# Attention into a squared-ReLU MLP on one core: contiguous scores in the first softmax, a single expansion of p for the late batches, and a new order of the work

## The chip, the cores and the metric

The kernel runs on one core of a Trainium2 chip. The metric is the device time of one execution in microseconds. Before the change, three runs took 312.1, 312.61 and 314.21 us; the median is 312.61 us. A profile of one further execution gives the durations used below.

## The reference

All inputs and the output are float32. There are 8 batches of 8 heads, 576 tokens, head dimension 64, and 32 packed queries `p` per head.

```python
def sm_attn(qq, kk, vv):
    s = scale * qq @ kk.T          # scale = 1/8
    a = exp(s - max(s)); a = a / (sum(a) + 1e-9)
    return a @ vv
p_packed = sm_attn(p, k, v)              # 32 packed queries over 576 keys
out = sm_attn(q, p_packed, p_packed)     # 576 queries over 32 packed keys
x = out.transpose(0, 2, 1, 3).reshape(4608, 512)
h = maximum(x @ w_in, 0)                 # 512 -> 2048
return (h * h) @ w_out                   # 2048 -> 512
```

## The kernel before, in words

**Steps of a batch.** GpSimd (POOL) issues all loads; they convert float32 to bfloat16 on the way. VectorE (DVE) transposes k and q in 32x32 blocks (`tr_k`, `tr_q`: Tk, Tq) and regroups v (`group`: G). Four heads are stacked on the 128 partitions; a `qd` is such a group of four heads, so a batch has two. `expand_p` (X) spreads the transposed p over a block-diagonal tile `pT_bd`, so that one matmul serves four heads.

S1 (`s1`, L467) multiplies p and k into PSUM, 128 rows by 576 scores. `s1_max` (L473, L474) takes the maximum and scales it, `s1_exp` (L481) does the exponential in two instructions (five and four groups of 32 keys a side) and spreads the result into the order in which v lies, with zeros behind it up to 640 columns. `s1_norm` (L489 to L491) adds the two sums, inverts them and normalises. E (`s1_tr`, `s1_out`: L496) transposes the result on PE and copies it out; PV (L509) multiplies it with v. XT copies the packed result out of PSUM twice: block-diagonally into `pq_bd` (`pq_block`) as the keys of the second attention, and into `ppT` (`extract`).

M (L532) multiplies the packed result with w_in, before the second attention's weights are applied; so the MLP's first product becomes a product of M and the attention weights. S2 (L553, and L560 for the last 64 tokens, `s2_rest`) computes the second attention's scores; L572 to L595 are its softmax; N (L602, L605) transposes it. F1 (L618) multiplies M and the weights in 16 blocks of 128 hidden units; each is rectified (L630 on ScalarE, or ACT; L632 on DVE) and squared (L640, or L638) into `gT`. F2 (L648) multiplies gT and w_out in 36 tiles of 128 tokens with 16 matmuls each; a tile is copied to `o_sb` and stored through the SyncE queue. L387 and L389 are the lines of the helper `cast`, which copies on ACT and on DVE.

**PSUM.** There are four tiles `ps0` to `ps3` of two banks each. S1, F1 and the large S2 take a whole tile (`HB`: ps0 or ps1). E, PV, the small S2 and N take one half of ps2 (`AB`: bank 4 or 5); M of batch 0 takes ps2 whole, later M takes ps2, ps0 or ps1. F2 takes one half of ps3 (`OB`: bank 6 or 7) in turn.

**The order.** Every engine works its instructions in the order in which the program emits them. `Plan` makes that order when the program is built: the work is given as streams of `Step`s, each with stages, the engines that may do them and an assumed duration. `forward` places one step after the other, that which could start first; a stream's number breaks near ties, and a step may be put into an earlier gap of its engine. `gate` keeps batch b's transposes and expansion behind F1 block 15 of batch b - 2. `plan.run(0, ())` takes the first order found. The functions `backward`, `vary` and `settle` aren't used by this call.

The lines that the steps of the prediction go back to are these, and the functions after them:

Of the kernel before, what the change touches and what calls it, by code (L numbers as in the profile page):

```python
# [3 lines left out]

# [11 lines left out]
P = 128  # L16
# [5 lines left out]
J0 = (0, 5, 10, 14)  # L22
FB = 128
WCH = 512
BDW = 384
# [5 lines left out]
class Piece:  # L31
    __slots__ = ("step", "stage", "k", "alts", "start", "end", "alt", "pred", "late", "order", "only")

    def __init__(self, step, stage, k, alts):
        self.step, self.stage, self.k, self.alts = step, stage, k, alts
        self.late = self.only = None


class Step:
# [4 lines left out]
    def __init__(self, name, segs, deps=(), take=(), give=(), lag=0.0, banks=(), free=()):  # L44
        self.name, self.deps, self.take, self.give, self.lag = name, list(deps), list(take), list(give), lag
        self.banks = list(banks)
        self.free_at = [[t or name for j, t in free if j == i] for i in range(len(segs))]
        self.pieces = [[Piece(self, i, k, p) for k, p in enumerate(st)] for i, st in enumerate(segs)]
        self.give_at = [[(p, t or name) for p, j, t in self.give if j == i] for i in range(len(segs))]


class Plan:
# [3 lines left out]
    def __init__(self, slots, nbanks):  # L56
        self.nslots, self.nbanks = slots, nbanks
        self.unit = {}
        self.streams, self.base = [], {}
        self.fill = 0  # L60

    def stream(self, prio, steps):
        self.streams.append((prio, list(steps)))

    def forward(self):

        busy = {e: ([-1.0], [t]) for e, t in self.base.items()}
        slots = {k: [] for k in self.nslots}
        last = {k: 0.0 for k in self.nslots}
        held, done, out = {}, {}, []  # L70
        banks = [(0.0, ())] * self.nbanks
        unit = {}
        pos = [0] * len(self.streams)
        since = [0.0] * len(self.streams)
        pend = []

        def ready(st, t):
            pred = []
            for d in st.deps:
                x = done.get(d)  # L80
                if x is None:
                    return INF, pred
                t = max(t, x[0] + HOP)
                pred.append(x)
            for p, n in st.take:
                s = slots[p]
                m = len(s) - self.nslots[p]
                for j in range(max(0, m), m + n):
                    x = s[j]
                    if x is None:  # L90
                        return INF, pred
                    t = max(t, x[0] + HOP)
                    pred.append(x)
                t = max(t, last[p])
            if st.banks:
                u = pick(st, t)
                if u is None:
                    return INF, pred
                for j in u:
                    t = max(t, banks[j][0] + HOP)  # L100
                    pred.append(banks[j])
            return t, pred

        def pick(st, t):
            best = None
            for k, u in enumerate(st.banks):
                if any(banks[j] is None for j in u):
                    continue
                x = max(t, max(banks[j][0] + HOP for j in u)) + 0.001 * k
                if best is None or x < best[0]:  # L110
                    best = (x, u)
            return best and best[1]

        def gap(e, us, t):

            s0, s1 = busy.setdefault(e, ([-1.0], [0.0]))
            i = bisect_right(s0, t) - 1
            t = max(t, s1[i])
            while i + 1 < len(s0) and s0[i + 1] < t + us - 1e-9:
                i += 1  # L120
                t = max(t, s1[i])
            return t, i

        def greedy(pc, t):
            if t == INF:
                return t
            b = None
            for e, us, _ in pc.alts:
                s = t if e == "-" else max(t, busy[e][1][-1] if e in busy else 0.0)
                if b is None or s + us < b[0]:  # L130
                    b = (s + us, s)
            return b[1]

        def book(e, t, f):
            s0, s1 = busy[e]
            i = bisect_right(s0, t) - 1
            if t - s1[i] < 1e-9:
                s1[i] = f
                if i + 1 < len(s0) and s0[i + 1] - f < 1e-9:
                    s1[i] = s1[i + 1]  # L140
                    del s0[i + 1], s1[i + 1]
            elif i + 1 < len(s0) and s0[i + 1] - f < 1e-9:
                s0[i + 1] = t
            else:
                s0.insert(i + 1, t)
                s1.insert(i + 1, f)

        while True:
            best = None
            for i, (prio, steps) in enumerate(self.streams):  # L150
                if pos[i] >= len(steps):
                    continue
                pc = steps[pos[i]].pieces[0][0]
                key = pc.late
                if best is not None and key is not None and key >= best[0]:
                    continue
                t, pred = ready(pc.step, since[i])
                if key is None:
                    key = greedy(pc, t) + 0.02 * prio
                if t < INF and (best is None or key < best[0]):  # L160
                    best = (key, pc, t, pred, i)
            for x in pend:
                key = x[0].late
                if key is None:
                    key = greedy(x[0], x[1]) + 0.02 * (x[2] - 0.5)
                if best is None or key < best[0]:
                    best = (key, x[0], x[1], x[3], x)
            if best is None:
                break
            _, pc, t, pred, src = best  # L170
            src_t = t
            b = None
            for i, (e, us, _) in enumerate(pc.alts):
                if (pc.only is None or pc.only == i):
                    s = t if e == "-" else gap(e, us, t)[0]
                    if b is None or s + us < b[0]:
                        b = (s + us, s, i, e)
            f, s, a, e = b
            pc.start, pc.end, pc.alt, pc.pred = s, f, a, pred
            if e != "-":  # L180
                book(e, s, f)
            out.append(pc)
            st = pc.step
            if pc.stage == 0:
                pos[src] += 1
                since[src] = s
                prio = self.streams[src][0]
                if st.banks:
                    u = unit[st.name] = pick(st, src_t)
                    for j in u:  # L190
                        banks[j] = None
                for p, k in st.take:
                    held[p, st.name] = range(len(slots[p]), len(slots[p]) + k)
                    slots[p] += [None] * k
                    last[p] = s
                ends = [pc]
            else:
                pend.remove(src)
# [719 lines left out]
```

## Time and profile before

| what | value |
|---|---|
| profiled execution | 313.22 us |
| its span | 311.5 us |
| PE busy | 249.4 us |
| DVE busy | 203.7 us |
| ACT busy | 183.1 us |
| POOL busy | 44.4 us |
| F2 matmuls (L648) | 576, 146.8 us |
| F1 matmuls (L618) | 512, 80.1 us |
| granted PE clock, mean | 0.99 |

Busy time of an engine is the time in which it has an instruction under way. A share of the span says little about one stage: the first 40 us and the last 35 us look different from the middle. An instruction's line is that of this kernel. In the timeline, a line gives start and duration in us, the engine, the line, output and input tiles, the count of merged instructions, and in brackets the idle time before it with what ended it. In the list of waits, "A <- B: t, n, m" says that A was idle for t us in n cases until B ended, the longest m us.

### The profile page before, as it was taken

The page shows a single profiled execution, that of the slowest core. Times are in us where ns is not written, and L with a number is a line of the kernel's source. Part 1 is how long each engine was busy: PE and PEld are TensorE (multiplying, and loading weights), DVE is VectorE, ACT ScalarE, POOL GpSimd, SP SyncE. Part 2 cuts the span into 40 slices and gives each one's busy share as a digit, 9 for nine tenths or more (in the row PEclk, how much of TensorE's full clock was granted, in tenths as well). Part 3 has the DMA queues.
Part 4 walks back from the last instruction along what each step waited for, and adds up shares of the span by engine and source line. Part 5 has one row for each costly group of instructions (what it writes and reads, how often), then busy time and mean ns, then how long its engine had stood idle before and what let it go on. Part 6 is the DMA issues. An engine that isn't in the chain of part 4 may idle for free.

```text
span 311.5 us, 5119 instructions
## 1 busy us (share of the span) xinstructions
PE 249.4 (80%) x1888; PEld 139.8 (45%) x1888; DVE 203.7 (65%) x437; ACT 183.1 (59%) x336; POOL 44.4 (14%) x76
## 2 busy tenths in 40 slices
PE   0243596799759888999899889988999799998883
PEld 0141254355526454655455444545454536653331
DVE  6658588879586957777778775786878575540000
ACT  1433287774877566757785767755885577751110
POOL 7655554304000300021000000000000000000000
PEclk9999999999997999999999999999999999999998
DMA  7999999997900691129411102020202111112222
GB/s 120 199 205 206 206 198 207 208 176 137 222 8 0 109 204 43 47 19 209 103 34 36 51 22 58 11 64 3 69 2 67 36 36 34 34 36 64 53 51 67
DMA packets 26456, 28.44 MB, mean 91 GB/s; under 512 B 5440, under 2 KB 17728, under 8 KB 26432
## 3 DMA queue, kind: packets, MB, share of 16 engines
q0 software_dynamic: 18992, 18.55, 37.6%
q1 hardware_dynamic: 6912, 9.45, 11.3%
q8 instruction: 14, 0.23, 0.3%
q10 hardware_dynamic: 528, 0.13, 0.2%
q14 instruction: 10, 0.08, 0.1%
HBM read 37.22 MB, written 9.44 MB: 150 GB/s over the span
## 4 chain that ended last, share of the span: by engine, by line
PE 59%; DVE 20%; ACT 11%; DMA 4%; issue 4%; POOL 1%; SPq 0%; ACTq 0%; DVEq 0%; POOLq 0%
PE ps L648 33%; PE ps L618 14%; ACT o_sb L387 5%; PE ps L553 2%; PE ps L467 2%; DMA v_b<-in_v_dram 2%; PE ps L532 2%; DVE pq_bd L389 2%; PE ps L602 2%; DMA out_dram<-o_sb 2%; DVE t L589 2%; DVE gT L640 2%; ACT pq_bd L387 2%; DVE n L595 1%; PE ps L509 1%
## 5 line engine op out<-in xcount | busy, mean ns | idle before, releaser
L648 PE MATMUL ps<-w_out_b,gT 128*128 128x512 bf16 x576 | 146.8, 380 | 15.9 <-ACT o_sb L387 14.2
L630 ACT ACTIVATE r<-ps 128x576 bf16<-128x576 f32 (+1 forms) x131 | 76.6, 617 | 19.5 <-PE ps L618 16.2
L648 PEld LDWEIGHTS <-gT 128*128 128x128 bf16 x576 | 54.4, 98 | 68.0 <-issue 17.1
L618 PE MATMUL ps<-a,M 128*128 128x288 bf16 x512 | 80.1, 292 | 5.9 <-ACT M L387 2.0
L618 PEld LDWEIGHTS <-M 128*128 128x128 bf16 x512 | 49.5, 99 | 33.6 <-issue 11.2
L640 DVE TENSOR_TENSOR gT<-r 128x576 bf16<-128x576 bf16 x119 | 51.9, 454 | 16.1 <-ACT r L630 15.0
L387 ACT COPY o_sb<-ps 128x512 f32<-128x512 f32 x32 | 18.8, 587 | 33.2 <-PE ps L648 33.2
L387 ACT CAST M<-ps 128x1024 bf16<-128x1024 f32 (+1 forms) x32 | 29.3, 958 | 14.2 <-PE ps L532 13.6
L481 ACT ACTIVATE e1x<-ps,n 128x320 bf16<-128x320 f32 (+1 forms) x32 | 25.3, 904 | 17.9 <-DVE n L474 17.9
L459 DVE STREAM_TRANSPOSE kT<-k_b 128x1152 bf16<-128x1152 bf16 x16 | 21.3, 1358 | 1.1 <-DMA k_b<-in_k_dram 1.1
L454 DVE STREAM_TRANSPOSE qT<-q_b 128x1152 bf16<-128x1152 bf16 x16 | 21.7, 1364 | 0.0
L467 PE MATMUL ps<-kT,pT_bd 128*128 128x288 bf16 x64 | 11.8, 313 | 11.3 <-DVE kT L459 11.1
L419 POOL DMA_DIRECT2D k_b<-in_k_dram x16 | 8.9, 554 | 72.5 <-DVE kT L459 66.1
L387 ACT COPY e<-ps 128x640 bf16<-128x640 bf16 x15 | 10.4, 692 | 12.3 <-PE ps L509 6.3
L389 DVE CAST pq_bd<-ps 32x64 bf16<-32x64 f32 x32 | 7.0, 219 | 14.7 <-ACT r L630 9.8
L532 PE MATMUL ps<-w_in_b,ppT 64*32 64x512 bf16 x256 | 11.5, 409 | 5.6 <-DVE M L389 2.9
L589 DVE TENSOR_REDUCE t<-e 128x36 f32<-128x1152 bf16 (+2 forms) x10 | 11.1, 1110 | 7.2 <-ACT e L583 7.2
L473 DVE TENSOR_REDUCE m<-ps 128x1 f32<-128x576 f32 x16 | 11.9, 742 | 4.6 <-PE ps L467 4.5
L467 PEld LDWEIGHTS <-pT_bd 128*128 128x128 bf16 x64 | 6.7, 104 | 16.5 <-issue 7.4
L572 DVE TENSOR_REDUCE m<-ps 128x4 f32<-128x128 f32 (+2 forms) x17 | 12.2, 719 | 2.1 <-PE ps L553 1.1
L427 POOL DMA_DIRECT2D v_b<-in_v_dram x18 | 12.2, 684 | 5.0 <-DMA k_b<-in_k_dram 1.8
L583 ACT ACTIVATE e<-d 128x1152 bf16<-128x1152 f32 (+2 forms) x10 | 9.7, 972 | 5.0 <-DVE d L577 4.9
(54 smaller groups left out, 197.9 us busy)
## 6 DMA issues: line engine op xcount, KB each, us to landing
out_dram<-o_sb SPq DMA_DIRECT2D x144, 64.0 KB, 1.7
k_b<-in_k_dram POOLq DMA_DIRECT2D x16, 288.0 KB, 8.4
q_b<-in_q_dram POOLq DMA_DIRECT2D x16, 288.0 KB, 10.3
v_b<-in_v_dram POOLq DMA_DIRECT2D x7, 320.0 KB, 10.3
w_in_b<-in_moe_w_in_dram POOLq DMA_DIRECT2D x8, 256.0 KB, 9.4
w_out_b<-in_moe_w_out_dram POOLq DMA_DIRECT2D x8, 256.0 KB, 10.3
v_b<-in_v_dram POOLq DMA_DIRECT2D x7, 256.0 KB, 10.6
v_b<-in_v_dram POOLq DMA_DIRECT2D x2, 160.0 KB, 6.6
```

Source lines behind the costliest of these rows:

```text
L387: nc.scalar.copy(dst, src)
L389: eng.tensor_copy(dst, src)
L454: nc.vector.transpose(self.qT[:, qd].rearrange("p dh (j a) -> p j dh a", a=32), self.t.q[qd][:].rearrange("p (j dh dl) -> p j dh dl", dh=2 ...
L459: nc.vector.transpose(kT[:, qd].rearrange("p dh (j a) -> p j dh a", a=32), self.t.k[qd][:].rearrange("p (j dh dl) -> p j dh dl", dh=2, dl=32))
L467: nc.tensor.matmul(ps[:, c], lhsT=pT_bd[self.b % 2][:, blk(qd, dh)], rhs=kT[:, qd, dh, c * HALF:(c + 1) * HALF], start=(dh == 0), stop=(dh ...
L481: nc.scalar.activation(e[:, i, :, :n], self.ps1[qd][:, :, x0 * 32:(x0 + n) * 32].rearrange("p c (x a) -> p c x a", a=32), ACT.Exp, bias=se ...
L532: nc.tensor.matmul(pair(u, j)[o:o + 32, qd, :], lhsT=self.ppT[64 * e:64 * e + 64, qd, pr, :], rhs=w_in_b[64 * e:64 * e + 64, qd * 2 + pr, ...
L589: nc.vector.tensor_reduce(self.t2[:, g0:g1], self.e2[:, g0:g1], axis=AX.X, op=ALU.add)
L618: nc.tensor.matmul(ps[:, c], lhsT=a.M[:, qd, fb * FB:(fb + 1) * FB], rhs=a.a2[:, qd, c * HALF:(c + 1) * HALF], start=(qd == 0), stop=(qd = ...
L630: nc.scalar.activation(dst, src, ACT.Relu)
L640: eng.tensor_tensor(out=Att.cols(gT[:, fb, o:o + S]), in0=r, in1=r, op=ALU.mult)
L648: nc.tensor.matmul(po[t], lhsT=gT[:, fb, n0:n0 + P], rhs=w_out_b[:, fb, :], start=(fb == 0), stop=(fb == NFB - 1))
```

## The change

Five things are edited together.

1. The first softmax. The columns of the score product are now written by S1 itself in the order of v: two pairs of matmuls with 256 columns and one pair with 64, whose moving operand is read in runs of 32 keys and whose output is written in runs of 64. The 576 scores of a row lie next to each other, so there is one maximum, one exponential of 576 columns with one sum, and no zero columns. The factor 1/8 is put into p when it is expanded, so the maximum isn't scaled. The last transpose of E takes the last 128 columns, of which the first 64 were transposed already; the matching rows of v are zeros.
2. `pT_bd` holds all eight batches. X.0 expands p for batches 0 and 1, X.1 once for batches 2 to 7, each in four pieces. POOL zeroes the late part (`setup2`, in the load queue behind the first four w_out loads, as I2).
3. Loads. Each k load becomes two, one per half of a row's tokens. v of batch 0 comes in two loads instead of four, and v's two parts take the lower and the upper 64 partitions instead of alternating ones. The identity is made after the loads of batch 0.
4. XT and S2. `extract` is two copies instead of four, each a piece of its own, and M waits for these two pieces alone. The large S2 stands before the small one in its stream. M may also be copied out by DVE, ReLU of batch 1 too.
5. The planner. `forward` now goes through time: at each moment the ready step with the lowest priority number takes its engine, and nothing is put into earlier gaps. Priorities come from a level per kind of step plus an offset per step from `TABLE`; `lean` shifts the choice between ACT and DVE. The durations of the steps are written anew.

The diff, cut to its core:

```diff
+    def forward(self):
...
+                cand.sort(key=lambda c: c[:2])
+                go = None
+                for pr, i, pc, x in cand:
+                    best = None
+                    for a, (e, us, _) in enumerate(pc.alts):
+                        b = t if e == "-" else max(t, busy.get(e, 0.0))
+                        v = b + us + (pc.step.lean if e == "ACT" else 0.0)
+                        if best is None or v < best[0]:
+                            best = (v, b, a, e, us)
+                    if best[1] > t + 1e-9:
+                        continue
...
+    def level(self, st):
+        c, b = (st.key.split(".") + ["0"])[:2]
+        c = c if c in self.levels else c[0]
+        return self.levels[c] + (10.0 * int(b) if c != "F2" else 10.0 * int(b) / 4.5)
...
+    def use(self, z):
+        level = {st.key: self.level(st) for steps in self.streams for st in steps}
+        self.prio = {k: level[k] + d for k, d in z.get("o", {}).items()}
+        self.lean = z.get("l", {})
+        self.wait, self.margin = z.get("w", 0.0), z.get("m", 0.0)
...
+TABLE = {'o': {'F1.1': -111.4, 'E.7': -15.38, 'F2.12': 29.55, 'F2.10': 62.36, 'PV.7': -8.82, 'Tk.5': -56.4, 'G.4':
...
+    60.11, 'F1.5': 20.76, 'F2.22': 41.33, 'E.4': -50.69, 'F2.4': 70.11, 'F1.0': 50.99, 'F1.3': 9.7, 'F1.4': -10.94,
+    'F1.6': -33.13, 'F1.7': 61.34, 'S1.7': -26.63, 'Tk.3': 10.86, 'G.0': 18.04, 'Tk.0': 0.11, 'S1.0': -5.5, 'E.0':
+    -43.01, 'PV.0': 24.59, 'M.0': 6.9, 'S2.0': -14.32, 'N.0': 3.07, 'F2.34': 79.86, 'F2.15': 128.64, 'Tk.4': -9.27,
...
-        e1x = consts.tile([P, NQD, (GM + 1) * P], BF16, name="e1x")
+        e1x = consts.tile([P, NQD, S], BF16, name="e1x")
-        pT_bd = [consts.tile([P, 896], BF16, name=f"pT_bd{i}") for i in range(2)]
+        pT_bd = consts.tile([P, B, NQD, 2, P], BF16, name="pT_bd")
...
+        def setup2():
+            nc.gpsimd.memset(pT_bd[:, 2:], 0.0)
+            for i in range(1, NV):
+                nc.gpsimd.memset(v_b[i][:64, :, GM * D:], 0.0)
...
+        def expand_p(b0, b1, h, eng):
+            dst = pT_bd[32 * h:32 * h + 32, b0:b1].rearrange("p b q dh c -> p (b q dh) c")[:, :, 32 * h:32 * h + 32]
+            src = pT[32 * h:32 * h + 32, b0 * NQD:b1 * NQD].rearrange("p n (dh i) -> p (n dh) i", i=NP)
+            if eng is nc.scalar:
+                nc.scalar.mul(dst, src, 0.125)
+            else:
+                eng.tensor_scalar_mul(dst, src, 0.125)
...
+                    src = k[self.b, qd * QH:(qd + 1) * QH].rearrange("h (j2 a x) d -> j2 h a (x d)", j2=2, x=VX)
+                    for j2 in range(2):
+                        nc.gpsimd.dma_start(t[:, j2 * VX * D:(j2 + 1) * VX * D], src[j2])
...
             def s1(self, qd, u):
-                ps = self.ps1[qd] = pair(u)[:, :, :HALF]
-                for c in range(2):
+                ps = self.ps1[qd] = pair(u).rearrange("p c n -> p (c n)")[:, :S]
+                kv = [kT[:, qd, dh].rearrange("p (j2 x a) -> p x j2 a", j2=2, a=32) for dh in range(2)]
+                w = [pT_bd[:, self.b, qd, dh] for dh in range(2)]
+                main = ps[:, :GM * P].rearrange("p (g i n) -> p i g n", i=2, n=64)
+                for i in range(2):
                     for dh in range(2):
-                        nc.tensor.matmul(ps[:, c], lhsT=pT_bd[self.b % 2][:, blk(qd, dh)],
-                                         rhs=kT[:, qd, dh, c * HALF:(c + 1) * HALF], start=(dh == 0), stop=(dh == 1))
+                        nc.tensor.matmul(main[:, i], lhsT=w[dh], rhs=kv[dh][:, i * GM:(i + 1) * GM],
+                                         start=(dh == 0), stop=(dh == 1))
+                for dh in range(2):
+                    nc.tensor.matmul(ps[:, GM * P:], lhsT=w[dh], rhs=kv[dh][:, 2 * GM], start=(dh == 0), stop=(dh == 1))
 
             def s1_max(self, qd):
-                self.tile_of("m1", small, [P, NQD], F32, bufs=2)
                 self.tile_of("n1", small, [P, NQD], F32, bufs=2)
-                nc.vector.tensor_reduce(self.m1[:, qd:qd + 1], self.ps1[qd], axis=AX.XY, op=ALU.max, negate=True)
-                nc.vector.tensor_scalar_mul(self.n1[:, qd:qd + 1], self.m1[:, qd:qd + 1], 0.125)
+                nc.vector.tensor_reduce(self.n1[:, qd:qd + 1], self.ps1[qd], axis=AX.X, op=ALU.max, negate=True)
 
             def s1_exp(self, qd):
...
+                nc.scalar.activation(e1x[:, qd], self.ps1[qd], ACT.Exp, bias=self.n1[:, qd:qd + 1],
+                                     accum_out=self.d1[:, qd:qd + 1])
...
+            def extract(self, e, eng):
+                self.tile_of("ppT", small, [P, NQD, 2, NP], BF16)
+                cast(eng, self.ppT[64 * e:64 * e + 64].rearrange("p qd pr i -> p (qd pr) i"),
+                     self.ps_pp[64 * e:64 * e + 64, :2 * P].rearrange("p (n i2 i) -> p n i2 i", i2=2, i=NP)[:, :, e])
...
-                res = [Step(nr, [r] + front(2, 128), pre, banks=AB, free=[(2, None)]),
-                       Step(nm, [a] + front(3, 1024), pre, banks=HB, free=[(2, None)]),
+                res = [Step(nm, [a] + front(3, 1024), pre, banks=HB, free=[(2, None)]),
+                       Step(nr, [r] + front(2, 128), pre, banks=AB, free=[(2, None)]),
                        Step(f"C.{b}", chain(4, 1152), [nm, nr])]
...
+        plan.levels.update(L=-99, I=-99, LP=-99, P=-9, X=-8, G=0, T=0, S1=1, E=1, PV=1, XT=1, S2=2, C=2, N=2, M=3, F1=15, F2=30)
...
+        ld += load_wo(range(0, 4)) + [Step("I2", [[[("POOL", 5.0, setup2)]]])]
+        ld += load_kq(1, "k") + load_v(1) + load_wo(range(4, 6)) + load_kq(1, "q") + load_wo(range(6, 8))
...
-        est = plan.run(0, ())
+        plan.use(TABLE)
+        est = plan.run()
```

The numbers of `TABLE` are an offset for each step; `F1.1` for instance stands for all F1 blocks of batch 1. The helpers `pick` and `ready` inside `forward` wait, as before, for a step's inputs, buffers and PSUM banks; they count the two banks of a PSUM tile as separate. `keep_clock`, called in `bank` and `pair`, emits nothing here, since `plan.fill` stays 0.

## The prediction

> **What bounds the kernel now.** I read the page's busy shares first, then the waits of PE, then head, middle and tail in the timeline.
>
> ```profile
> PE 249.4 (80%) x1888; PEld 139.8 (45%) x1888; DVE 203.7 (65%) x437; ACT 183.1 (59%) x336; POOL 44.4 (14%) x76
> PE   0243596799759888999899889988999799998883
> DVE  6658588879586957777778775786878575540000
> ```
>
> PE is the busiest engine, and its slices are full except in the first eighth, around the tenth slice and in the last. So the question is what becomes of the 311.5 - 249.4 = 62.1 us in which PE is idle. The waits of PE say whom it waited for (total, times, longest):
>
> ```profile
> PE ps L648 <- ACT o_sb L387: 14.2, 23, 0.7
> PE ps L467 <- DVE kT L459: 11.1, 2, 8.5
> PE ps L560 <- DVE ppT L389: 6.2, 6, 1.6
> PE ps L496 <- DVE e1n L491: 3.5, 3, 3.0
> PE ps L532 <- DVE M L389: 2.9, 2, 1.4
> PE ps L532 <- DVE d L577: 2.6, 2, 2.2
> PE ps L560 <- ACT ppT L387: 2.1, 1, 2.1
> ```
>
> Asked for the stretch before the first F1 matmul at 37.59 us alone, these waits sum to 26.4 us: the **head**. Behind it PE waits 14.5 us for output copies (14.2 ACT, 0.3 DVE), 8.3 us for ppT (6.2 + 2.1), and 7.9 us for a dozen small things, nearly all between 37.6 and 118 us; after its last matmul 5.0 us pass. 26.4 + 14.5 + 8.3 + 7.9 + 5.0 = 62.1. From 132.5 to 262.9 us (four batches, 32.6 us each) PE is busy 119.0 us of 130.4: a wait of 2.9 us a batch is all that any order could still win there.
>
> The head, on VectorE:
>
> ```profile
> 7.08 1.38 DVE L459 STREAM_TRANSPOSE kT<-k_b 128x1152 bf16<-128x1152 bf16 x1 [1.07 <-DMA k_b<-in_k_dram]
> 10.42 0.49 DVE L389 COPY v_g<-v_b 128x1280 bf16<-128x1280 bf16 x1 [1.97 <-DMA v_b<-in_v_dram]
> 10.83 1.37 DVE L459 STREAM_TRANSPOSE kT<-k_b 128x1152 bf16<-128x1152 bf16 x1
> 12.13 0.72 DVE L473 TENSOR_REDUCE m<-ps 128x1 f32<-128x576 f32 x1
> ```
>
> VectorE stands 1.97 us for a load of v that the order put ahead of the second half of k, though the second k transpose, when its turn comes, waits for no DMA. PE's second S1, both maxima, both exps and all behind them start late by that.
>
> The tail and every change of an F2 tile:
>
> ```profile
> 280.81 0.58 ACT L387 COPY o_sb<-ps 128x512 f32<-128x512 f32 x1 [2.59 <-PE ps L648]
> 281.44 3.61 PE L648 MATMUL ps<-w_out_b,gT 128*128 128x512 bf16 x16 [0.67 <-ACT o_sb L387]
> ```
>
> The next tile writes the other half of the same two-bank tile (OB), and PE still waits for the copy: 0.67 us wherever two F2 tiles follow each other directly.
>
> **The change, part by part.**
>
> *Head, to the second softmax (S2.0, now 22.23 us).* In the new order both k transposes are ready before v. VectorE then does kT at 7.1 to 8.5 and 8.5 to 9.9, if k's second half is there; the extra 2 x 0.55 us of POOL issue for the split k loads (0.554 us a DMA) stand ahead of it, so 0 to 1.1 us later. The copy of v (0.49) and its ScalarE twin (1.26) move behind. That wins up to 10.83 - 8.5 = 2.3 us, less 0 to 1.1; I take 1.5. The first softmax then loses one exp of two. Two exps and their accumulator reads take 1.37 us a pass (13.13 to 14.50). One contiguous exp of 576: the exp of 512 took 0.63 and of 1152 took 1.165, a line that gives 0.68; the ReLU of 576 from PSUM took 0.65. With the read (0.27) 0.95; 0.4 saved a pass, two passes, 0.8. The scale of the negated maximum (L474, 0.154) and the addition of the two sums (L489, 0.138) go, twice each: 0.6. Sum 2.9. Against it, S1 issues six matmuls for four, with the same 1152 columns, but with moving operand and output in strided runs. No row shows such a read; I bound it from nothing to a doubling of S1 (0.49 a pass warm: four starts from 203.67 to 204.16), and take 0.05 a pass, since columns decide in the other rows. About 2.8 us to S2.0.
>
> *Head, S2.0 to F1.0 (now 22.23 to 37.59, 15.4 us).* VectorE runs 24.3 to 35.4 nearly without a hole, and 4 x 0.69 us of it are halves of M that ScalarE does in 0.58. PE's transposes of the softmax then wait for the last of these halves ("PE ps L602 <- DVE M", 1.4), because both use the ps2 tile. The new table ranks the softmax of batch 0 above its M. I take half of the 2.8 us and the 1.4: 2.8. The bounds are 0, since M still shares ps2, and 5. Head in sum: **-5.6 us**, between -1 and -9. What is late next there is VectorE itself: transposes of q (2 x 1.37), norms and copies fill 8.5 to 18 us, so I don't follow the sum to its lower end.
>
> *ppT.* Now the small S2 matmul (L560) stands first on PE and waits for pq_block on both engines, then for ppT, because its bank lies in the same ps2 tile. The diff puts the large S2 first, which needs the pq blocks only; L560 follows 1.0 us later. The four ppT casts (0.73 us) leave PE's path and become two. Seven waits of 1.19 shrink by up to 0.73: -5.1. But the blocks are still cast one engine after the other (0.92, then 0.84), and PE waits for the second; if the order puts S2 earlier than now, the wait returns. I take **-4**, between -6 and +4.
>
> *The small waits from 37.6 to 118 us (7.9 us).* There VectorE and ScalarE are as busy as PE (8.5, 8.4 us of ten). A batch loses on VectorE 2 x (0.154 + 0.138) + about 0.4 for two ppT casts + up to 0.8 for expand_p (four copies of 0.204), some 1.5 of 24.4 us, and on ScalarE 2 x 0.4 of 22. I take **-2.5**, between -6 and +4 (another order can make these waits too).
>
> *Output copies.* OB and its two banks stay, so each direct change of tile still costs 0.67. Now 24 of 35 changes cost it; a new order can make it 15 or all 35. I take **0**, between -6 and +7.
>
> *Off the path, at nothing.* The late batches' expand (X.1) and the zeroing on POOL (setup2) lie in the load queue ahead of the k loads of batch 1. By POOL's 0.543 us for 512 elements, 3072 and 3 x 512 elements cost 3.3 + 1.6 = 4.9 us. Sixteen split k loads add 8.9 us of issue over the kernel, and dropping batch 0's v from four to two loads takes 1.3 away. POOL is 14% busy, and kT of batch 1 (issued at 21.3, landing in about 10.3) starts at 37.9 us: 6 us of cover now, hardly any once the head is 5.6 shorter. Price if the cover goes: up to 5 us, once. The traced rows show no VectorE instruction slowed beside a POOL memset (a kT transpose takes 1.37 us beside the one at 37.89).
>
> The Trainium skill, "SBUF — State Buffer", section "SBUF: two separate sides", speaks against this piece: GpSimd and some VectorE modes share a port pair as an exclusive lock, and the loser stands for the whole instruction. By that rule a 3.3 us memset could hold a VectorE copy as long, and the head would win 3.3 us less; the row above, an instruction outside those modes perhaps, can't decide it.
>
> *PE's own work* is unchanged but for S1: +1.
>
> *Sum:* -5.6 - 4 - 2.5 + 0 + 1 = -11.1, a span of 300.4. The profiled execution took 313.22, 1.7 over its span: 302.1. It lies 0.6 above the median of the runs shown (312.61), so I say **301.5 us**.
>
> **Rivals.**
>
> *The order wins more.* If it also separates F2 tiles by other matmuls (-6) and the head reaches -9, the sum is -20: 292, down to 284. For it: the idle time is there, 62 us of it. Against: the tail's eight direct changes have no other work to part them.
>
> *The head's gain is given back.* F1 starts earlier, but PE then waits for k, q, w_out or VectorE; -5.6 becomes 0, and ppT's -4 is met by +4 in another place: 309 to 313. For it: slices five to thirteen, where VectorE and ScalarE are already near nine tenths.
>
> *Slower: PE's queue stops at its head.* PE works in order; a batch puts eleven small groups (S1, transposes, PV, S2, M) between F matmuls. Each that stands a little too early holds all F work behind it, and the planner still lets a half of ps2 or ps3 be written while the other is read, which the kernel doesn't (0.67 above; "DVE pq_bd" after "ACT pq_bd"). Half a PSUM copy (0.3 us of 0.6) for each of eleven is 3.3 us a batch, 23 over seven: 301.5 + 23 = 324. It decides from 1.6 us a batch on (11.1 over seven), against 2.9 now. For it: the priorities are scattered so that neighbours of a batch stand far apart. Against: many F matmuls are ready at most times, and the durations written into the steps are near the rows here.
>
> *It doesn't do what it says.* Strided S1 reads cost a doubling (16 x 0.49 = 8) and the exp doesn't get shorter: 308 to 311.
>
> **How the numbers follow.** Forecast case (295 to 308) 0.50; more won (284 to 295) 0.17; given back or no use (308 to 313) 0.16; slower (313 to 326) 0.17. The lower bounds of all terms together would be under 284, the upper ones about 320; 285 to 317 leaves out some 0.05 below and 0.10 above. One per cent is 3 us, about what a measurement of this kernel can tell from no change: faster than 309.5 takes the first two cases and a third of the third, 0.72; within 1% 0.12; slower 0.16.
>
> **What would show it.** The second kT transpose by 9.5 us; one exp of 128x576 per pass at 0.7 us; S2.0 near 19.5 and F1.0 near 32; ppT gone from PE's waits, replaced by pq_bd under 0.6 each; o_sb still at 0.67 a wait; a batch of 31 to 32 us in the middle. It is wrong if the batch grows above 33 with PE waiting for pq_bd, e1n or M, or if F1.0 comes early and the gain is lost by 118 us.

## The result

Six runs of the changed kernel took 309.06 to 311.48 us, with a median of 310.44; six runs of the kernel before beside them took 312.1 to 314.21, median 312.89. The ratio is 0.9915, with a 95% interval of 0.9892 to 0.9938. The change wins some 2.7 us where 11 were forecast. The profiled execution has a span of 309.2 us (before: 311.5).

The first three views of the changed kernel's page: busy times, and two of the rows in 40 slices.

```profile
PE 251.5 (81%) x1920; PEld 143.4 (46%) x1920; DVE 202.3 (65%) x370; ACT 163.8 (53%) x298; POOL 59.7 (19%) x91
PE   0244459769899899999999998899999898998883
DVE  3667457888998856877997589765788456364000
```

ScalarE loses 19.3 us of work (183.1 to 163.8) and VectorE 1.4. PE, which sets the time, is still below full in the first eighth; VectorE's first digit fell from 6 to 3, so VectorE stands idle for most of the first slice. The waits of PE (total, times, longest) say what it stood for:

```profile
PE ps L409 <- DVE kT L398: 14.6, 3, 11.3
PE ps L590 <- ACT o_sb L318: 11.8, 20, 0.7
PE ps L433 <- DVE e1n L427: 6.6, 4, 2.2
PE ps L590 <- DVE o_sb L320: 3.2, 6, 0.8
PE ps L474 <- DVE d L519: 2.1, 1, 2.1
PE ps L495 <- ACT pq_bd L318: 1.8, 1, 1.8
PE ps L560 <- ACT r L572: 1.7, 4, 0.7
```

(S1 is L409 now, E L433, M L474, S2 L495, F1 L560, F2 L590.) ppT is gone. In its place stand longer waits for kT (11.1 before) and for e1n (3.5 before), and ReLU ("r"). Split as in the prediction, by asking for the stretches before and after the first F1 matmul, with the version "whole rows" of the first experiment beside it (its profiled execution took 304.67 us, 2.0 less than its median). The wait right before the first F1 matmul counts to the head in all three columns.

| PE, us | before | changed | whole rows |
|---|---|---|---|
| start of S2.0 | 22.23 | 22.49 | 18.70 |
| start of F1.0 | 37.59 | 39.10 | 35.22 |
| head: waits up to F1.0 | 26.4 | 26.5 | 22.6 |
| behind it: output copies | 14.5 | 15.0 | 15.0 |
| behind it: S2, for ppT before, for ReLU now | 8.3 | 0.2 | 0.0 |
| behind it: other waits | 7.2 | 10.4 | 10.9 |
| after the last matmul | 5.0 | 5.1 | 5.1 |
| not listed | 0.7 | 0.5 | 0.6 |
| busy | 249.4 | 251.5 | 248.7 |
| span | 311.5 | 309.2 | 302.9 |

From the middle column, the order did win 8.1 us at S2. It gave 3.2 of them to other waits and 0.5 to output copies, PE was busy 2.1 longer, and the head won nothing in place of 5.6. So the first question is the head. There VectorE shows:

```profile
9.90 1.38 DVE L398 STREAM_TRANSPOSE kT<-k_b 128x1152 bf16<-128x1152 bf16 x1 [5.87 <-DMA k_b<-in_k_dram]
11.51 1.38 DVE L398 STREAM_TRANSPOSE kT<-k_b 128x1152 bf16<-128x1152 bf16 x1 [0.22 <-DMA k_b<-in_k_dram]
12.81 0.72 DVE L416 TENSOR_REDUCE n<-ps 128x1 f32<-128x576 f32 x1
```

The copy of v no longer stands between the transposes, as forecast. But VectorE waits 5.87 us for the first load of k and starts on it at 9.90 us, where it could start at 7.08 before. That uses up what the order and the shorter softmax win up to S2.0.

### The profile page after: what moved, and what is told of

Its sections match the earlier page's. It is cut to its first block, busy times and chain, and to the rows that moved or that the text cites. A ratio compares the mean times of both kernels' runs of the same rounds, so it can differ in the third digit from the quotient of the medians.

```text
span 309.2 us, 5088 instructions
## 1 busy us (share of the span) xinstructions
PE 251.5 (81%) x1920; PEld 143.4 (46%) x1920; DVE 202.3 (65%) x370; ACT 163.8 (53%) x298; POOL 59.7 (19%) x91
## 4 chain that ended last, share of the span: by engine, by line
PE 65%; DMA 12%; ACT 9%; DVE 8%; issue 3%; POOL 1%; ACTq 0%; DVEq 0%; POOLq 0%
PE ps L590 38%; PE ps L560 17%; ACT o_sb L318 4%; DMA w_in_b<-in_moe_w_in_dram 3%; DMA q_b<-in_q_dram 3%; DMA w_out_b<-in_moe_w_out_dram 3%; DMA k_b<-in_k_dram 2%; ACT r L572 2%; PE ps L474 2%; PE ps L495 2%; PE ps L409 2%; DVE o_sb L320 1%; PE ps L544 1%; PE ps L433 1%; PE ps L447 1%
## 5 line engine op out<-in xcount | busy, mean ns | idle before, releaser
L590 PE MATMUL ps<-w_out_b,gT 128*128 128x512 bf16 x576 | 148.2, 380 | 15.0 <-ACT o_sb L318 11.8
L560 PE MATMUL ps<-a,M 128*128 128x288 bf16 x512 | 83.4, 293 | 4.7 <-ACT r L572 1.7
L590 PEld LDWEIGHTS <-gT 128*128 128x128 bf16 x576 | 54.0, 98 | 62.8 <-issue 17.0
L560 PEld LDWEIGHTS <-M 128*128 128x128 bf16 x512 | 50.1, 100 | 39.7 <-issue 15.2
L318 ACT COPY o_sb<-ps 128x512 f32<-128x512 f32 x27 | 15.8, 586 | 42.3 <-PE ps L590 38.3
L361 POOL DMA_DIRECT2D k_b<-in_k_dram x32 | 22.3, 703 | 38.8 <-DVE qT L393 22.7
L318 ACT CAST M<-ps 128x1024 bf16<-128x1024 f32 (+1 forms) x28 | 24.2, 896 | 10.4 <-PE ps L474 10.4
L409 PE MATMUL ps<-kT,pT_bd 128*128 128x256 bf16 x64 | 11.3, 307 | 14.8 <-DVE kT L398 14.6
L420 ACT ACTIVATE e1x<-ps,n 128x576 bf16<-128x576 f32 x16 | 11.9, 744 | 11.1 <-DVE n L416 8.3
L416 DVE TENSOR_REDUCE n<-ps 128x1 f32<-128x576 f32 x16 | 11.9, 745 | 5.7 <-PE ps L412 5.7
L474 PE MATMUL ps<-w_in_b,ppT 64*32 64x512 bf16 x256 | 11.2, 402 | 5.1 <-DVE d L519 2.1
L409 PEld LDWEIGHTS <-pT_bd 128*128 128x128 bf16 x64 | 6.3, 106 | 18.0 <-issue 9.6
L357 POOL DMA_DIRECT2D q_b<-in_q_dram x16 | 8.9, 560 | 25.4 <-DVE qT L393 18.7
L433 PE MATMUL ps<-ident,e1n 128*128 128x128 bf16 x80 | 8.2, 241 | 6.9 <-DVE e1n L427 6.6
L318 ACT COPY a<-ps 128x576 bf16<-128x576 bf16 x12 | 7.4, 640 | 11.7 <-PE ps L547 8.4
## 6 DMA issues: line engine op xcount, KB each, us to landing
p_b<-in_p_dram POOLq DMA_DIRECT2D x1, 192.0 KB, 10.4
```

The costliest lines, as they stand in the source:

```text
L318: nc.scalar.copy(dst, src)
L361: nc.gpsimd.dma_start(t[:, j2 * VX * D:(j2 + 1) * VX * D], src[j2])
L409: nc.tensor.matmul(main[:, i], lhsT=w[dh], rhs=kv[dh][:, i * GM:(i + 1) * GM], start=(dh == 0), stop=(dh == 1))
L416: nc.vector.tensor_reduce(self.n1[:, qd:qd + 1], self.ps1[qd], axis=AX.X, op=ALU.max, negate=True)
L420: nc.scalar.activation(e1x[:, qd], self.ps1[qd], ACT.Exp, bias=self.n1[:, qd:qd + 1], accum_out=self.d1[:, qd:qd + 1])
L474: nc.tensor.matmul(pair(u, j)[o:o + 32, qd, :], lhsT=self.ppT[64 * e:64 * e + 64, qd, pr, :], rhs=w_in_b[64 * e:64 * e + 64, qd * 2 + pr, ...
```

## The experiments

Each run has the time of the kernel before, taken on the same chip, beside it.

**1. Whole rows: the changed kernel with k loaded as before.** Only `dma_kq` and `dma_v` differ from the changed kernel; k, and v's two parts, are read so that one row of 18 tokens is one piece again (k in two loads a batch instead of four, v in four instead of two), and the softmax and the order stay.

```diff
-                    src = k[self.b, qd * QH:(qd + 1) * QH].rearrange("h (j2 a x) d -> j2 h a (x d)", j2=2, x=VX)
-                    for j2 in range(2):
-                        nc.gpsimd.dma_start(t[:, j2 * VX * D:(j2 + 1) * VX * D], src[j2])
+                src = {"k": k, "q": q}[name]
+                nc.gpsimd.dma_start(t, src[self.b, qd * QH:(qd + 1) * QH].rearrange("h (a j) d -> (h a) (j d)", j=JT))
...
-                src = v[self.b].rearrange("h (ap x) d -> ap h (x d)", x=VX)
-                nc.gpsimd.dma_start(self.v_raw[64 * i:64 * i + 64, :, :n * D], src[:, :, i * GM * D:(i * GM + n) * D])
+                src = v[self.b].rearrange("h (a j2 x) d -> j2 a h (x d)", j2=2, x=VX)
+                for j2 in range(2):
+                    p0 = 64 * i + 32 * j2
+                    nc.gpsimd.dma_start(self.v_raw[p0:p0 + 32, :, :n * D], src[j2][:, :, i * GM * D:(i * GM + n) * D])
```

> The changed kernel with k loaded in whole rows again, one load per group of four heads; v then comes in four loads of 32 partitions instead of two of 64, and nothing else is edited, the order of the work included. Theory (the shape of the k loads is what ate the head's gain): no 4-byte packets beyond some 1100, the first kT transpose at 7.1 to 7.6 us instead of 9.9, S1 of batch 1 without the 2.8 us wait for kT, F1.0 at 34 to 36 us instead of 39.1, and 304 to 307 us in time against 310.4. Rival (the order on PE is what ate it, the loads are covered later): kT at 7.5 but F1.0 still behind 38 and 309.5 to 311.

Measured: 306.64 us (304.67 to 307.12), ratio 0.9798 [0.9761, 0.9835], 3.8 us under the changed kernel's median. VectorE's timeline:

```profile
6.19 2.79 DVE L396 STREAM_TRANSPOSE kT<-k_b 128x1152 bf16<-128x1152 bf16 x2 [2.32 <-DMA k_b<-in_k_dram]
8.91 0.72 DVE L414 TENSOR_REDUCE n<-ps 128x1 f32<-128x576 f32 x1
```

Both transposes are done at 8.98, not 12.89; S2.0 starts 3.79 us earlier, F1.0 3.88, and the whole is 3.8 shorter. So the head was lost in the loads. That it was k's: v is issued only from 4.11 us on in the changed kernel, when k is late already, and neither there nor here does VectorE wait for v of batch 0. One expectation wasn't met: S1 of batch 1 still waits for its kT (2.72 us, 2.81 in the changed kernel). What the DMA engines moved in the first 16 us shows it too (40 slices of 0.4 us; first the changed kernel, then whole rows):

```profile
GB/s 0 0 0 0 43 237 49 15 2 1 16 29 55 60 55 58 89 107 82 121 119 159 183 169 188 180 202 192 202 206 203 204 212 223 209 190 213 224 190 209
```

```profile
GB/s 0 0 0 0 41 246 86 40 109 190 190 190 207 196 207 147 187 195 180 190 194 192 213 223 203 227 196 213 225 185 195 189 139 141 195 205 210 200 205 207
```

From 2.8 to 6.4 us, when nothing but k, v and q is under way, the changed kernel moves 1 to 60 GB/s where whole rows move 40 to 207.

**2. The kernel before with each k load halved.** The same count of loads as the change has, but each half is a plain two-dimensional block (128 rows by half a row's columns), not four heads by 32 rows by half a row.

```diff
+                src = src[self.b, qd * QH:(qd + 1) * QH].rearrange("h (a j) d -> (h a) (j d)", j=JT)
+                m = JT * D // 2
+                for x in range(2 if name == "k" else 1):
+                    c = slice(x * m, x * m + m) if name == "k" else slice(0, 2 * m)
+                    nc.gpsimd.dma_start(t[:, c], src[:, c])
```

> The kernel before with one edit: each k load becomes two loads of half a row (1152 bytes a row in SBUF), with the old assignment of tokens, so that each half is still a two-dimensional pattern of 128 equal rows. Theory A (halving the load is what costs): kT starts at 9 to 10 us instead of 7.1, thousands of 4-byte packets more, and 2 to 4 us more in time. Theory B (the four-head, 32-row pattern of the changed load is what costs, not the halving): kT within 0.6 us of 7.1 plus the extra issue of 0.55, no 4-byte packets more, time within 1 us of 312.6.

Measured: 312.94 us (312.65 to 315.21), ratio 1.0022 [0.9998, 1.0047]. The first kT transpose waits for no load:

```profile
5.96 1.38 DVE L462 STREAM_TRANSPOSE kT<-k_b 128x1152 bf16<-128x1152 bf16 x1
```

In runs 3, 4 and 8, which load k as before, it starts at 6.05 to 6.23 us, so the 7.08 of the first profile is on the late side. Two loads for one cost nothing that can be seen; the four-head form does. The page's line of packets points to what is different about it (changed kernel, then before):

```profile
DMA packets 41016, 28.50 MB, mean 92 GB/s; under 512 B 17952, under 2 KB 34336, under 8 KB 40992
```

```profile
DMA packets 26456, 28.44 MB, mean 91 GB/s; under 512 B 5440, under 2 KB 17728, under 8 KB 26432
```

Counted by size, the packets of the queue in which GpSimd issues are:

```
                      4 B    1152 B    2304 B
before               1072         0      4096
changed             13584      4096      2048
whole rows           1296         0      4096
before, k halved     1328      4096         0
```

(Other sizes, the weights' among them, are left out.) The four-head form adds 13584 - 1296 = 12288 packets of 4 bytes: 32 loads of 128 rows make 4096 rows, so three to each. It also takes longer to issue: 2.86 us for the four loads of batch 0, where the halved loads of run 2 took 2.26.

The records of single packets in the traces show what differs. The first four packets of the four-head load start at 2.82 to 2.92 us and the fifth at 4.15. From 3.2 to 4.0 us four packets of k are under way at a time, where whole rows and the kernel before have 16 and the halved loads 17; from 4.4 to 5.2 us, with further loads begun, there are 8. So the first load of this form has as many packets under way as it has heads, and a quarter of what the other forms have. The packets of 4 bytes fit this: the other three versions have 16 to a load (67, 81 and 83 loads), and the four-head load has 384 more, which is 12 x 32, as if 12 of the 16 DMA engines got 32 of them each while four carried 32 rows each. That is a reading of the counts; the records used here don't tell the engines apart.

That the form costs the time is shown by runs 1 and 2, and the trace shows few packets under way as the difference; the slower issue is 0.6 us of it at most.

**3. The kernel before with the large S2 ahead of the small one.** Batches 1 to 7; the small S2 and what belongs to it are put behind the large one in the emitted order, nothing else moves.

```diff
+        for b in range(1, 8):
+            for stage, behind in (0, 0), (1, 2), (2, 2):
+                x = at[f"S2.{b}.1", stage]
+                todo.remove(x)
+                y = todo.index(at[f"S2.{b}.0", behind] if stage < 2 else at[f"S2.{b}.1", 1])
+                todo.insert(y + 1, x)
```

> The kernel before with its own order, only that for batches 1 to 7 the large S2 stands before the small one on PE, and the same for the maximum and the subtraction behind them on VectorE. Theory (ppT's place was worth what the prediction's step said): PE's 8.3 us of waiting for ppT fall to under 2, and the time falls by 2 to 5 us. Rival (PE then waits for the pq blocks or for F1's PSUM tiles, and the gain is given back): ppT's wait goes, but the time is within 1 us of 312.6.

Measured: 314.09 us (311.8 to 315.81), ratio 1.0038 [1.0007, 1.0070]. No wait for ppT is left, and these are new (waits of PE; L561 is the large S2 here):

```profile
PE ps L561 <- ACT r L638: 3.6, 6, 1.5
PE ps L561 <- DVE r L640: 1.9, 1, 1.9
```

The large S2 takes ps0 or ps1, which F1 fills in turn, and now waits until ReLU has read F1's scores: of 8.3 us, 5.5 come back at S2. The ppT wait was cover for that one: taken away alone, with the order around it left as it was, it brings no gain.

**4. The kernel before with its new first softmax alone.** The contiguous scores, one exponential and 1/8 in p; k in whole rows, the order, the expansion per batch and the copies of XT as before.

```diff
-        e1x = consts.tile([P, NQD, (GM + 1) * P], BF16, name="e1x")
+        e1x = consts.tile([P, NQD, S], BF16, name="e1x")
...
-                cast(eng, bd2(pT_bd[b % 2], h), pT[32 * h:32 * h + 32, b * NQD:(b + 1) * NQD].rearrange(
-                    "p q (two i) -> p q two i", two=2))
+                eng.tensor_scalar_mul(bd2(pT_bd[b % 2], h), pT[32 * h:32 * h + 32, b * NQD:(b + 1) * NQD].rearrange(
+                    "p q (two i) -> p q two i", two=2), 0.125)
```

(`s1` to `s1_norm` are those of the change.)

> The kernel before, in its own order, with the first softmax of the change alone: scores in v's order with 576 contiguous columns, one maximum, one exp, 1/8 folded into p. k is loaded in whole rows as before; v comes in loads of 32 partitions, twice as many. Theory (less work on ScalarE and VectorE hardly moves a PE-bound kernel): one exp of 0.75 us a pass, S1 0.1 us a pass longer, time 1 to 3 us below 312.5, nearly all of it before 45 us. Rival (the softmax's saving is what the changed kernel's gain consists of): 5 us or more below. Second rival (the doubled v loads cost the head as much as the softmax wins): within 1 us of 312.5.

Measured: 312.19 us (310.43 to 313.1), ratio 0.997 [0.9945, 0.9995]. ScalarE is busy 171.4 us for 183.1, F1.0 starts at 36.08 for 37.59, of which 1.0 is k's earlier arrival (6.08 for 7.08), and the kernel gains some 0.9 us. VectorE's second transpose still stands behind v:

```profile
9.14 0.59 DVE L389 COPY v_g<-v_b 128x1280 bf16<-128x1280 bf16 x1 [1.68 <-DMA v_b<-in_v_dram]
9.65 1.36 DVE L460 STREAM_TRANSPOSE kT<-k_b 128x1152 bf16<-128x1152 bf16 x1
```

Runs 1 and 4 part the change into three, taken in this order: the softmax 0.003 of the time, 0.9 us; from there to whole rows (0.997 to 0.9798, the new order with the single expansion, XT's two copies and the rest, which no run takes apart) 5.4 us; the load of k (0.9798 to 0.9915) -3.7 us. The sum, 2.6, is the change's 0.0085; the intervals leave each part open by about 1 us.

**5. Whole rows, zeroing moved out of the load queue.** Zeroing pT_bd's late part follows the last w_out load, and that of v goes to the identity's place, both away from the k loads of batch 1.

```diff
-            nc.gpsimd.memset(pT_bd[:, 2:], 0.0)
-            for i in range(1, NV):
-                nc.gpsimd.memset(v_b[i][:64, :, GM * D:], 0.0)
...
+            if c == 7:
+                setup2()
```

> The kernel of the first experiment (k in whole rows, 306.6 us) with POOL's 4.2 us of zeroing taken out from in front of batch 1's k loads: the v buffers are zeroed behind the identity, the late part of pT_bd behind the last w_out load. Theory (the DMA engines were full all the time, so the load queue's pause cost nothing): batch 1's first kT stays within 0.7 us of 30.6 and the time within 1 us of 306.6. Rival (the zeroing holds back k of batch 1, for which PE waits 2.7 us): kT 2 us or more earlier, 303 to 305.

Measured: 306.41 us (305.87 to 306.85), ratio 0.9796 [0.9761, 0.9831], the same as whole rows; kT of batch 1 starts at 30.04 us for 30.61, though its load is issued at 19.93 for 24.00. The loads already issued keep the DMA engines busy while GpSimd zeroes: in whole rows they move 205 GB/s from 20.0 to 24.2 us. It was not tried to put the k loads of batch 1 ahead of the w_out loads before them in the queue.

**6 and 7. Whole rows, F1 of batch 0 ahead of S1 of batch 1.** In whole rows PE stands at S1 of batch 1 while work of batch 0 lies behind it:

```profile
32.04 1.01 PE L407 MATMUL ps<-kT,pT_bd 128*128 128x256 bf16 x4 [2.72 <-DVE kT L396]
32.85 0.31 PE L410 MATMUL ps<-kT,pT_bd 128*128 128x64 bf16 x2
32.97 0.61 PE L542 MATMUL ps<-ident,n 128*128 128x128 bf16 x4
...
35.22 0.80 PE L558 MATMUL ps<-a,M 128*128 128x288 bf16 x4 [0.39 <-ACT e1x L418]
```

(L542 is N.0.1, L558 F1.0.) Both versions put N.0.1 and F1.0.0 to F1.0.2 earlier in the emitted order; the second also holds back Tk, S1 and E of batch 1.

```diff
+        early = [p for p in todo if p.step.name == "N.0.1" or p.step.name in [f"F1.0.{i}" for i in range(3)]]
+        todo = [p for p in todo if p not in early]
...
-        todo[i:i] = early
+        todo = [p for p in todo[:i] if p not in hold] + early + hold + todo[i:]
```

> The kernel of the first experiment with one move in the order: the second transposition of batch 0's softmax (N.0.1) and the first three F1 blocks of batch 0 stand, on every engine, ahead of batch 1's first k transpose, S1 and softmax, behind which they stood; all else keeps its order. Theory (PE's queue stops at S1 of batch 1 while F1 of batch 0 is ready): F1.0 starts at 30 to 31 us instead of 35.2, PE's 2.7 us of waiting for kT fall under 1, and the time falls by 1.5 to 4 us, to 302.5 to 305. Rival (the ramp is bound by what VectorE, ScalarE and the loads deliver, not by the place in PE's queue): F1.0 early, but within 1 us of 306.6.

Measured: 307.26 us (306.96 to 307.54), ratio 0.9824 [0.9793, 0.9856]. The first S1 of batch 1 still stood ahead of N.0.1, so F1.0 came 1.6 us earlier (33.59), and the wait for e1n grew from 7.1 to 8.1. The second version made the move whole.

> The changed kernel with k in whole rows, with the second half of batch 0's softmax transposes (N.0.1) and F1 blocks 0 to 2 of batch 0 ahead of all of S1 of batch 1 and of E of batch 1. Theory: in the version with whole rows alone PE stands 2.7 us at S1 of batch 1 for its k transpose while F1 of batch 0 could run; with S1 behind three F1 blocks (1.2 us each), F1 starts at 32 to 33 us instead of 35.2 and 1.5 to 2.5 us of the 306.64 go: 304 to 305. Rival: the chain behind S1 of batch 1 (maximum, exponential, normalisation, E) sets the time by then, and the wait for e1n grows by what F1 starts earlier, as it did by 1.0 us where the move took effect in part: 306 to 308.

Measured: 307.05 us (305.62 to 307.72), ratio 0.9807 [0.977, 0.9845]: F1.0 at 30.55 us, 4.7 earlier, and no gain. PE's timeline and VectorE's:

```profile
30.55 3.35 PE L565 MATMUL ps<-a,M 128*128 128x288 bf16 x12
36.18 1.04 PE L414 MATMUL ps<-kT,pT_bd 128*128 128x256 bf16 x4 [2.28 <-DVE kT L403]
```

```profile
34.01 0.46 DVE L579 TENSOR_SCALAR r<-ps 128x288 bf16<-128x288 f32 x1 [6.70 <-PE ps L565]
34.39 0.45 DVE L587 TENSOR_TENSOR gT<-r 128x576 bf16<-128x576 bf16 x1
34.75 2.63 DVE L403 STREAM_TRANSPOSE kT<-k_b 128x1152 bf16<-128x1152 bf16 x2
```

F1's ReLU came along on VectorE and stands ahead of the k transposes, so these start at 34.75 for 30.61, and S1 of batch 1 at 36.18 for 32.04: 4.1 us later. What F1 wins, batch 1's softmax loses, at its k transpose and not, as the rival had it, by longer waits for e1n (6.4 us for 7.1). It was not tried to let VectorE transpose first.

**8, 9 and 10. F2's two banks as two tiles.** In place of ps3 with two banks there are two PSUM tiles of one bank each; banks, order and instructions stay.

```diff
-        ps = [psum.tile([P, 2, 512], F32, name=f"ps{i}") for i in range(4)]
+        ps = [psum.tile([P, 2, 512], F32, name=f"ps{i}") for i in range(3)]
+        po_t = [psum.tile([P, 512], F32, name=f"po{i}") for i in range(2)]
```

With the kernel before:

> The kernel before with one edit: the two banks that F2 uses in turn are two PSUM tiles of one bank each instead of the halves of one tile. The order is untouched. Theory (the 0.67 us at each change of F2 tile is the shared tile and nothing else): the 14.5 us that PE waits for output copies go to under 1, and the time falls by 9 to 14 us, to 299 to 304. Rival (the waits move to the softmax steps, which set the pace of a batch): the wait goes, other waits of PE grow by as much, and the time falls by less than 4 us.

Measured: 294.46 us (294.01 to 295.53), ratio 0.9425 [0.9398, 0.9452]. No wait for o_sb is left. In the end stretch of PE's timeline the changed kernel does one tile after another with a pause, and the two-tile version of before runs through. The third view is ScalarE's in the two-tile version:

```profile
287.83 3.61 PE L590 MATMUL ps<-w_out_b,gT 128*128 128x512 bf16 x16 [0.67 <-ACT o_sb L318]
292.12 3.61 PE L590 MATMUL ps<-w_out_b,gT 128*128 128x512 bf16 x16 [0.67 <-ACT o_sb L318]
296.41 3.61 PE L590 MATMUL ps<-w_out_b,gT 128*128 128x512 bf16 x16 [0.67 <-ACT o_sb L318]
```

```profile
263.44 23.90 PE L649 MATMUL po<-w_out_b,gT 128*128 128x512 bf16 x110
```

```profile
270.11 0.59 ACT L388 COPY o_sb<-po 128x512 f32<-128x512 f32 x1 [2.87 <-DMA out_dram<-o_sb]
273.57 0.59 ACT L388 COPY o_sb<-po 128x512 f32<-128x512 f32 x1 [2.87 <-DMA out_dram<-o_sb]
```

From one tile to the next is 4.29 us with the pause; without it 16 matmuls take 3.46, by which the o_sb copies of the two-tile version follow each other. So such a change of tile costs 0.83, not the listed 0.67: 0.16 of it, the last matmul's end, which PE would overlap with the next one, counts as busy. Before's 24 waits are listed with 14.5 in all, not all of full length; with 24 x 0.16 they make 18.3, and 18.1 were won.

With whole rows:

> The kernel of the first experiment with F2's two banks as two PSUM tiles of one bank each. Theory (the same cost of the shared tile stands in the changed kernel, and the new order doesn't lessen it): PE's 15.0 us of waiting for output copies go to under 1 and the time falls by 10 to 15 us, to 291.5 to 296.5. Rival (the new order has less other work at those places, so the waits turn up elsewhere): 298 to 303.

Measured: 287.7 us (286.49 to 288.09), ratio 0.9190 [0.9156, 0.9223], 18.9 us under whole rows. This is the fastest version here, faster than both kernels.

With whole rows and the move of run 7:

> The same order with F2's two banks as two PSUM tiles of one bank each. Theory: both gains are of different places, so they add: 287.7 less 1.5 to 2.5, that is 285 to 286.5. Rival: 287 to 289.

Measured: 288.18 us (287.95 to 288.3), ratio 0.9213 [0.9195, 0.9231]: the move is worth nothing here either.

## Why the prediction was wrong

The forecast was a span shorter by 11.1 us; the profiles show 2.3. The head fell short by 5.7 us, the small waits by 5.7, output copies and PE's own work by 1.6, and ppT won 4.1 more than forecast.

**Head, to S2.0: forecast -2.8, measured +0.3. This is the step that failed first.** Its order part was right: both transposes stand before v, one exponential of 576 takes 0.74 us. Its term "0 to 1.1 later" for the split k loads was mis-sized: the kT transposes start 3.7 and end 3.9 us later than with whole rows (12.89 against 8.98), and S2.0 3.8 later (22.49 against 18.70). I priced the loads by their count, at POOL's issue; run 2 shows that the count is free, and runs 1 and 2 that the form costs 3.7 us of the whole time. With whole rows S2.0 is at 18.70, where 19.5 was forecast.

**Head, S2.0 to F1.0: forecast -2.8, measured +1.2** (15.36 to 16.61 us), and +1.2 with whole rows too, so this has another cause. What I did look at, VectorE and the halves of M, came out as forecast: from S2.0 to the first transposes of the softmax (N.0.0) it was 13.18 us before and is 9.88 now. The first line below is from before's chain that ended last (start, duration, engine, tile, line), the others are from PE's timeline now.

```profile
35.41 0.58 PE ps L602 x4
```

```profile
32.37 0.59 PE L544 MATMUL ps<-ident,n 128*128 128x128 bf16 x4 [1.19 <-ACT M L318]
35.92 1.01 PE L409 MATMUL ps<-kT,pT_bd 128*128 128x256 bf16 x4 [2.81 <-DVE kT L398]
```

I did not look at which work of batch 1 the new order sets in this stretch: N.0.1 and F1 stand on PE behind S1 of batch 1, which waits 2.8 us for its k. Run 7 shows that this term was of little worth in any case: with F1.0 4.7 us earlier nothing is won, since batch 1's softmax is then as much later. "The head's gain is given back" describes this part.

**ppT: forecast -4, measured -8.1 (8.3 to 0.2).** The mechanism was right in the new order and the size too small. The fear that PE would then wait for pq_block did not come true: there is one such wait, in batch 0 (1.8 us, in the head), and it was 1.7 before. But run 3 shows that the edit I named, S2 ahead, doesn't win this by itself; the new order also has ReLU done by then.

**Small waits behind the first F1: forecast -2.5, measured +3.2 (7.2 to 10.4).** VectorE and ScalarE did lose work, as worked out, but the waits grew. Those of E for e1n went from 0.5 to 3.4 us, and all of these are batch 1's, directly behind the first F1:

```profile
42.15 0.71 PE L433 MATMUL ps<-ident,e1n 128*128 128x128 bf16 x5 [1.94 <-DVE e1n L427]
46.27 0.71 PE L433 MATMUL ps<-ident,e1n 128*128 128x128 bf16 x5 [1.48 <-DVE e1n L427]
```

Whole rows has the same two (1.36 and 2.42). I read that as the order's doing, which puts E of batch 1 where its e1n isn't ready; no run takes this apart, so the cause stays open. The upper bound of +4 held. Two readings that stood behind this term and behind the rival of the lost gain were off: "8.5, 8.4 us of ten" for VectorE and ScalarE holds for 40 to 50 us alone (7.9 and 7.1 of ten from 40 to 118 us), and slices five to thirteen are not near nine tenths (digits 5 to 9 for VectorE, 2 to 8 for ScalarE). And the sum that gave 62.1 has one wait of 0.7, that right before F1.0, both in the head and in the 7.9.

**Output copies: forecast 0, measured +0.5.** 26 waits for 24. That these were the one place worth 18 us, in both kernels, lay outside the change; the prediction had their sum and priced each at 0.67, where a full one cost 0.83. The Trainium skill, "PSUM — Partial Sum Buffer", section "PSUM bank collisions raise a hardware error", says that engines' accesses to different banks run clean. Run 8 agrees: in it one bank is written while the other is read, and 18.1 us are gone.

**Zeroing in the load queue: forecast 0, measured 0** (run 5), for another reason than POOL's idle time: the DMA engines had enough in hand. It took 4.2 us for 4.9. VectorE's instructions beside the memset of 2.68 us kept their 0.68 to 0.69 us; those were reductions and subtractions that read PSUM, so copies are not tested.

**PE's own work: forecast +1, measured +2.1,** which doesn't tell much. An S1 pass went from 0.49 to 0.58 us (the starts 77.84 and 78.42), 16 x 0.09 = 1.4. But the seven profiles of versions with the changed kernel's matmuls have PE busy between 248.0 and 252.3 us. The same matmuls are also not equally fast everywhere: in the changed kernel four of F1 take 1.17 us at 48.16 and 0.65 at 49.56, in the kernel before 0.65 already at 44.68. No run takes this apart.

**The rivals.** "The order wins more" was not it. "Slower" did not come. The time, 310.44, lies in the case "given back or no use" (308 to 313, 0.16), by a mixture: the head not won, small waits given back. Without the load's form the change would be at 306.6, in the forecast case's upper part.

## What to carry to other kernels

When a load is split, price the form of each piece, not only the count: look in the trace for how fast the first bytes of that form arrive and how many packets are under way, and where nothing shows the form, let its bound be as wide as the load's whole latency. A wait that PE loses is won only if what stood second in line is ready too, and a step moved forward brings its instructions on the other engines along: list those before pricing the move. Wait for the halves of a buffer as separate tiles when producer and consumer alternate between them.

## What the runs showed of the hardware

A load of four heads by 32 rows by half a row (1152 bytes) into 128 partitions has three extra 4-byte packets a row, has four packets under way at a time at its start where plain two-dimensional blocks have 16 or 17 (3.2 to 4.0 us), and arrives late: VectorE could start on its k at 9.90 us, against 5.96 to 7.08 with plain blocks of a whole or half a row.

The listed idle time before a matmul (0.67 us) was less than what the wait cost (0.83 us), because the end of the matmul before it counts as busy.
